# Experts' weights split into high and low parts in the experts' stage instead of beforehand, and position scatters in a chain

## The chip, the core and the metric
One Trainium2 chip, one of its cores. The metric is the device time of one execution in microseconds. Engines: PE (TensorE, matrix products), PEld (its weight loads), DVE (VectorE), ACT (ScalarE), POOL (GpSimd), SP (SyncE, which here issues nearly all DMAs).

## What is computed
Three layers in a row over 8 batches of 576 tokens, 4608 tokens of 512 numbers, all in 32-bit floating point.

```python
p_packed = sm_attn(p, k, v)                  # 32 packed queries per head attend to the keys
out = sm_attn(q, p_packed, p_packed)         # every token attends to the 32 packed rows
h = x @ w_in;  g = h * sigmoid(h);  x = g @ w_out          # 512 -> 2048 -> 512
e_idx = argmax(x @ w_gate)                                 # one of 8 experts for each token
gate = softmax(x @ w_gate)[e_idx] * sigmoid(x @ w_output_gate)[e_idx]
for e in range(8):                                         # 512 -> 1024 -> 512
    out[mask] = gate[mask] * (relu(x[mask] @ w1[e]) @ w2[e])
```

## The kernel before
**Products from two parts.** A matrix product in full precision is made of three products of rounded operands: a number is kept as a part rounded to the chip's type fp32r (hi) and the rest (lo), and lo x hi, hi x lo and hi x hi are summed in PSUM. Making the two parts of a tile takes two instructions: a copy on ACT that rounds (hi), and a subtraction on DVE (lo). This text calls the pair a rounding.

**Batches.** The first two layers run batch by batch (`batch`, L358). A batch has 16 steps, one for each 128 of the 2048 inner features. Step f issues in this order: the first product of step f (`mm1`, L690, into the PSUM buffer ps_h, of which there is one), the activation (`act`: tanh on ACT at L699, product g on DVE at L700, which frees ps_h), parts of other work by a schedule (`extra_steps`: attention of the next batch in pieces s1 to s9, the product m of the next weights with its m_lo at L672, and the routing of the batch before), the rounding of g (L705, L710, L717, L719), and the second product of step f-2 (`mm2`, L741). Every engine works through its own instructions in this order. In routing, `row_t` transposes the finished rows, `row_logits` and `row_logits2` make the experts' logits (the copy of lg at L290 reads ps_h), `finish` finds the best expert (mx, L764) and queues the gate's weights, and `place` works out each token's position among those of its expert and scatters token numbers there.

**Weights of the experts, beforehand.** From batch 1 to 6, `split_slot` (L505) is called in two of three steps: it takes a piece of w1 or w2 (128x1024, 512 KB) that SP has loaded, rounds it (ACT at L509, DVE at L510), and issues the load of another piece (`split_load`). `split_store` at the head of the next step writes both parts to the DRAM tensors ws1 and ws2. There are 64 pieces: 8 experts, two matrices, four pieces.

**Experts.** Tokens are handled in groups of 576 that have one expert; here there are 8 groups. Each group has 8 steps of 128 inner features, 64 steps in all, n = 0 to 63 (`groups`, L902). In step n the order is: up-projection of n+1 (`up`, L1011 on PE, relu at L1016 on ACT and its lo part at L1017 on DVE, again through one buffer ps_h), gap 2n+1, down-projection of n (`down`, L1033, L1036), gap 2n+2. A gap is a list of jobs put there by hand or by `plan`: transposes of the next group's rows (`trx`, L975 to L981), fetching the group after it (`fetch`: its expert's number, the token numbers from the DRAM table perm at L924 and L925, then five gathers of rows on POOL at L934), and loads of weights. `load_chunk` (L953) loads a quarter of an expert's weights, hi and lo of both matrices, 2 MB in two issues on SP (L959, L961), into a ring of five buffers; two belong to the pool qa, open since batch 7, three to the pool p2, which lies on memory of the batches and is opened as the experts begin. Chunks 0 and 1 are loaded in step 2 of batch 7 (`open_first`). The first group takes tokens of the first batches only, so its fetch begins in step 1 of batch 7.

**Position scatters.** `place` (L784) issues one indirect DMA on POOL for each 128 tokens (L809), 36 in all, four or five at a time. Before each one POOL clears a small tile (`spacer`), and `rows_apart` declares that they need not wait for each other. The loads at L924 and L925 read what they wrote. Four of the scatters are issued as the last batch ends and one in gap 3 of the experts.

Of the kernel before, what the change touches and what calls it, by code (L numbers as in the profile page):

```python
# [21 lines left out]
DM = 512  # L22
# [18 lines left out]
RING = 5  # L41
# [46 lines left out]
class Kernel:  # L88
    def __init__(self, tc, ins, out):
        self.tc, self.nc, self.i, self.out = tc, tc.nc, ins, out  # L90
        nc = tc.nc
        self.ws1 = nc.dram_tensor("ws1", (E8, 4, 2, 128, F2), F32, kind="Internal").ap()
        self.ws2 = nc.dram_tensor("ws2", (E8, 4, 2, 128, 2 * DM), F32, kind="Internal").ap()
        self.perm = nc.dram_tensor("perm", (PROWS, PW), I32, kind="Internal").ap()
        self.xr = nc.dram_tensor("xr", (NTOK + 1, XW), F32, kind="Internal").ap()
# [5 lines left out]
    def run(self):  # L101
# [19 lines left out]
        self.spacer = cp.tile([128, 1], I32, name="spacer")  # L121
# [16 lines left out]
        self.split_jobs = [(w, e, k) for e in range(E8) for w in (1, 2) for k in range(4)]  # L138
        self.split_n, self.split_raw, self.split_loaded, self.split_done = 0, [], [], []
        self.late, self.group = [], None  # L140
        self.ex, self.at, self.x, self.sc, self.hl, self.chunk = {}, {}, {}, {}, {}, {}
        self.xt, self.nload, self.banks = [None, None], 0, 2
# [6 lines left out]
        c_stg, self.stg = self.pool("spl", "right")  # L149
        for b in range(1, B - 1):  # L150
            self.batch(b)
        while self.split_jobs or self.split_loaded or self.split_done:
            self.split_store()
            self.split_slot()
        c_stg.close()
# [47 lines left out]
    def open_first(self, f):  # L203
        nc = self.nc
        if f == 1:
            self.ex[0] = nc.values_load(self.ptab[0:1, 0:1], engines=[ENG.SP], min_val=0, max_val=E8 - 1)
            xs = [self.p1.tile([128, 2, S], F32, tag=f"a2_0{i}", name="xs") for i in range(2)]
            self.fetch_ix(0, self.ptab[0:1, 1:2])
            og = xs[1][:, 1, :DM]
            nc.sync.dma_start(og, self.i["wog"][bass.ds(self.ex[0], 1), :].to_broadcast([128, DM]))  # L210
            mid = self.mid[:, 2 * DM:2 * DM + 2 * XW].rearrange("p (a b) -> p a b", a=2)
            self.x[0] = [*(x[:, :XW] for x in (xs[0][:, 0], xs[0][:, 1], xs[1][:, 0])), mid[:, 0], mid[:, 1]], og
        elif f == 2:
            self.load_chunk()
            self.load_chunk()
        elif f == 4:
            self.fetch_x(0)
        elif f == 13:
            t = self.pin.tile([128, 4 * FF], F32R, tag="w_in", name="xt0")
            self.xt[0] = t[:, :8 * GN].rearrange("p (h k t) -> p h k t", h=2, k=4)  # L220
            self.ring = t[:, 8 * GN:14 * GN].rearrange("p (i t) -> p i t", i=3)
# [136 lines left out]
    def batch(self, b, hook=None):  # L358
        sched = self.extra_steps(b)
        for f in range(NF):  # L360
            s = b * NF + f
            self.split_store()
# [13 lines left out]
            slot = 0 < b < B - 1 and (s - NF) % 3 < 2  # L376
            if slot and f != 1:
                self.split_slot()
# [3 lines left out]
            if slot and f == 1:  # L382
                self.split_slot()
# [18 lines left out]
            if b == 0 and f == 15:  # L402
                self.split_load()
                self.split_load()
# [92 lines left out]


    def split_store(self):
        for w, hi, dst in self.split_done:  # L500
            self.nc.sync.dma_start(dst[0], hi.bitcast(F32))
            self.nc.sync.dma_start(dst[1], w)
        self.split_done = []

    def split_slot(self):  # L505
        nc = self.nc
        for w, dst in self.split_loaded[:1]:
            hi = self.stg.tile([128, 1024], F32R, tag="shi", bufs=2, name="shi")
            nc.scalar.copy(out=hi, in_=w)  # L509
            nc.vector.tensor_tensor(out=w.bitcast(F32R), in0=w, in1=hi.bitcast(F32), op=ALU.subtract)  # L510
            self.split_done.append((w, hi, dst))
        self.split_loaded = self.split_loaded[1:]
        self.split_load()

    def split_load(self):
        nc = self.nc
        if not self.split_jobs:
            return
        which, e, k = self.split_jobs.pop(0)
        n = self.split_n  # L520
        self.split_n += 1
        if n < 3:
            self.split_raw.append(self.mid[:, (n + 1) * 1024:(n + 2) * 1024])
        elif n == 3:
            self.split_raw.append(self.stg.tile([128, 1024], F32, name="sw"))
        w = self.split_raw[n % 4]
        if which == 1:
            nc.sync.dma_start(w, self.i["w1"][e].rearrange("(k p) f -> p k f", p=128)[:, k, :])
            dst = self.ws1[e, k]
        else:  # L530
            nc.sync.dma_start(w.rearrange("p (k d) -> p k d", k=2),
                              self.i["w2"][e].rearrange("(k p) d -> p k d", p=128)[:, 2 * k:2 * k + 2, :])
            dst = self.ws2[e, k]
        self.split_loaded.append((w, dst))
# [249 lines left out]
    def place(self, g):  # L784
# [15 lines left out]
        def put():  # L800
# [6 lines left out]
            for r in range(n):  # L807
                nc.gpsimd.memset(self.spacer, 0)
                put = nc.gpsimd.indirect_dma_start(  # L809
                    out=self.perm, out_offset=bass.IndirectOffsetOnAxis(ap=di[:, r:r + 1], axis=0),  # L810
                    in_=self.tok[:, i0 + r:i0 + r + PW], in_offset=None)
                self.rows_apart("perm", put.ins)
# [57 lines left out]
    def more(self, lo, hi):  # L870
        self.nload = 4 * lo
        self.fetch(lo)
        for _ in range(4):
            self.load_chunk()
# [10 lines left out]
    def plan(self, lo, hi, first=5, every=2):  # L885
        for k in range(lo, hi - 1):
# [15 lines left out]
    def groups(self, lo, hi):  # L902
        self.gap(2 * FG * lo)
        for n in range(FG * lo, FG * hi):
# [10 lines left out]
            if n % 2 and n > 6 and self.nload < 4 * hi:  # L915
                self.load_chunk()
# [36 lines left out]
    def load_chunk(self):  # L953
        nc, n = self.nc, self.nload
        self.nload += 1
        slot, e, q = n % RING, self.expert(n // 4), n % 4
        t = (self.qa if slot < 2 else self.p2).tile([128, 4096], F32R, tag=f"w{slot}", name="w")
        f = t.bitcast(F32)
        nc.sync.dma_start(f[:, :2048].rearrange("p (a c) -> p a c", a=8),  # L959
                          self.ws1[bass.ds(e, 1), :, :, :, q * 256:q * 256 + 256].rearrange("e a b p c -> p (e a b) c"))  # L960
        nc.sync.dma_start(f[:, 2048:].rearrange("p (b c) -> p b c", b=2), self.ws2[bass.ds(e, 1), q].rearrange("e b p c -> p (e b) c"))  # L961
        self.chunk[n] = t
# [57 lines left out]
    def down(self, n, parts=None):  # L1020
# [3 lines left out]
        for n, j in parts:  # L1024
            g, ff = divmod(n, FG)
            w = self.chunk[n // 2][:, 2048:].rearrange("p (r k c) -> p r k c", r=2, k=2)[:, :, ff % 2, :]
# [65 lines left out]
```

## Time and profile before

| | us |
|---|---|
| median of 3 runs (lowest, highest) | 1271.96 (1271.86, 1272.64) |
| the profiled execution's own time | 1271.73 |
| its span, first to last instruction | 1269.6 |
| batches 1 to 6, about 140 to 736 us | 596 |
| batch 7 and the last rows, 736 to 834 us | 98 |
| experts, from 834 us | 425 to the last products, then 10 |

Mean granted clock of TensorE over the span: 0.984 of full speed. In the profile, L12 is line 12 of the kernel before; a name such as `acc<-wo,ghi` is the tile written and the tiles read. In a timeline a line is one instruction or several merged ones (x8): start in us from the span's first instruction, duration, engine, line, tiles, shape. What stands in brackets is the time that the engine had nothing to do before it and the instruction that ended that time; no bracket means no idle time. SPq lines are issues of DMAs. In the windows view a line is a stretch: its length, the busy us of PE, PEld, DVE, ACT and POOL with their numbers of instructions, the granted TensorE clock as a share of full speed, the mean busy share of the 16 DMA engines, and GB/s. A step number is f in `batch`; batches count from 0.

### The profile page before, as it was taken

What the parts mean: (1) busy time and instruction counts of PE and PEld (TensorE: products, weight loads), DVE (VectorE), ACT (ScalarE), POOL (GpSimd) and SP (SyncE); (2) the same over time, 40 slices, a digit from 0 to 9 for tenths busy, and PEclk for the clock granted to TensorE, in tenths of its full rate; (3) what the DMA queues carried; (4) which work ended last, traced back from release to release, by engine and by line L of the source; (5) the groups of instructions that cost most, each with busy time, mean ns of one, the idle gap of its engine ahead of it and who ended that gap; (6) DMA issues with size and microseconds to landing.
All of it is one profiled execution on the core that took longest, in us unless ns stands there. A gap on an engine that the chain in (4) does not pass through costs nothing. (4 is left out here: it accounts for less than half of the span.)

```text
span 1269.6 us, 22035 instructions
## 1 busy us (share of the span) xinstructions
PE 1204.2 (95%) x8760; PEld 998.4 (79%) x8760; DVE 656.2 (52%) x1495; ACT 472.9 (37%) x978; POOL 168.9 (13%) x211
## 2 busy tenths in 40 slices
PE   7697999999999999999999899999999999999996
PEld 3575887787777787787788778888999999999996
DVE  6889657456657556756645834433233232322311
ACT  3433554354554454464444433312221212212121
POOL 0234201000101000100000131013311303111011
PEclk9797999999999999999999999999999999999998
DMA  8555566565766656875845551069755656565411
GB/s 312 205 185 180 178 239 215 197 238 194 257 243 194 234 189 219 240 261 171 280 172 215 162 181 35 2 176 354 264 182 204 231 188 227 180 232 196 173 38 40
DMA packets 118725, 250.26 MB, mean 197 GB/s; under 512 B 13363, under 2 KB 64374, under 8 KB 118358
## 3 DMA queue, kind: packets, MB, share of 16 engines
q1 hardware_dynamic: 111318, 228.66, 53.1%
q0 software_dynamic: 7296, 20.11, 4.2%
q8 instruction: 71, 1.16, 0.4%
q14 instruction: 40, 0.33, 0.1%
HBM read 160.17 MB, written 88.70 MB: 196 GB/s over the span
## 5 line engine op out<-in xcount | busy, mean ns | idle before, releaser
L741 PE MATMUL acc<-wo,ghi 128*128 128x512 f32 x1024 | 320.7, 394 | 0.0
L741 PEld LDWEIGHTS acc<-wo,ghi 128*128 128x128 f32 x1024 | 194.4, 190 | 38.9
L1011 PE MATMUL pu<-xt,w 128*128 128x256 f32 (+1 forms) x1536 | 215.5, 296 | 0.0
L1011 PEld LDWEIGHTS pu<-xt,w 128*128 128x128 f32 x1536 | 209.6, 189 | 5.1
L741 PE MATMUL acc<-wo,glo 128*128 128x512 f32 x512 | 213.1, 416 | 0.0
L690 PE MATMUL ps_h<-a,m_hi 128*128 128x288 f32 x1024 | 212.1, 300 | 0.8 <-DVE a L656 0.8
L1017 DVE SCALAR_TENSOR_TENSOR xt<-pu,xt 128x512 fp32r<-128x512 f32 (+1 forms) x128 | 58.7, 458 | 294.9 <-ACT xt L1016 287.9
L1036 PE MATMUL py<-w,xt 128*128 128x512 f32 x768 | 187.7, 393 | 0.0
L690 PE MATMUL ps_h<-a,m_lo 128*128 128x288 f32 x512 | 161.8, 316 | 24.1 <-DVE g L700 17.2
L1016 ACT ACTIVATE xt<-pu 128x512 fp32r<-128x512 f32 (+1 forms) x128 | 52.7, 412 | 324.4 <-PE pu L1011 274.2
L1036 PEld LDWEIGHTS py<-w,xt 128*128 128x128 f32 x768 | 144.3, 188 | 33.0
L690 PEld LDWEIGHTS ps_h<-a,m_hi 128*128 128x128 f32 x1024 | 168.1, 193 | 2.5 <-DVE a L656 1.0
L700 DVE SCALAR_TENSOR_TENSOR g<-g,ps_h 128x576 f32<-128x576 f32 x128 | 96.1, 751 | 131.2 <-ACT g L699 130.8
L699 ACT ACTIVATE g<-ps_h 128x576 f32<-128x576 f32 x128 | 83.4, 652 | 171.8 <-PE ps_h L690 155.3
L690 PEld LDWEIGHTS ps_h<-a,m_lo 128*128 128x128 f32 x512 | 98.4, 192 | 50.4 <-DVE g L700 26.1
L741 PEld LDWEIGHTS acc<-wo,glo 128*128 128x128 f32 x512 | 97.3, 190 | 46.0 <-issue 27.0
L809 POOL DMA_INDIRECT perm<-tok,dsti x36 | 39.5, 1098 | 653.0 <-DVE dsti L805 516.7
L710 DVE TENSOR_TENSOR glo<-g,ghi 128x512 fp32r<-128x512 f32 x128 | 91.5, 715 | 38.2 <-ACT ghi L705 33.7
L705 ACT CAST ghi<-g 128x512 fp32r<-128x512 f32 x128 | 79.4, 620 | 74.1 <-DVE g L700 71.2
L510 DVE TENSOR_TENSOR mid<-mid,shi 128x1024 fp32r<-128x1024 f32 x48 | 58.8, 1226 | 43.3 <-ACT shi L509 43.3
L561 PE MATMUL ps_m<-w_in,ppt 64*32 64x256 f32 x1008 | 44.7, 399 | 9.2 <-ACT e L577 5.3
L509 ACT CAST shi<-mid 128x1024 fp32r<-128x1024 f32 x48 | 50.1, 1045 | 0.0
(188 smaller groups left out, 1155.8 us busy)
## 6 DMA issues: line engine op xcount, KB each, us to landing
w<-ws SPq DMA_DIRECT2D x64, 1024.0 KB
ws<-shi SPq DMA_DIRECT2D x64, 512.0 KB
mid<-in_w SPq DMA_DIRECT2D x48, 512.0 KB
ws<-mid SPq DMA_DIRECT2D x48, 512.0 KB
att_v<-in_v SPq DMA_DIRECT2D x15, 640.0 KB
att_k<-in_k SPq DMA_DIRECT2D x15, 576.0 KB
xr<-xr SPq DMA_DIRECT2D x32, 256.5 KB
stg<-in_w_in SPq DMA_DIRECT2D x16, 512.0 KB
```

The lines of the kernel that those rows point to most:

```text
L509: nc.scalar.copy(out=hi, in_=w)
L510: nc.vector.tensor_tensor(out=w.bitcast(F32R), in0=w, in1=hi.bitcast(F32), op=ALU.subtract)
L690: nc.tensor.matmul(ps[:, hf, :288], lw[:, qd, fs], rx[:, qd, ts], start=(i == 0), stop=(i == 5))
L699: nc.scalar.activation(out=g2, in_=ps[:, :, :288], func=AF.Tanh, scale=0.5)
L700: nc.vector.scalar_tensor_tensor(out=g2, in0=g2, scalar=1.0, in1=ps[:, :, :288], op0=ALU.add, op1=ALU.mult)
L705: self.nc.scalar.copy(out=hi, in_=self.graw[:, :512])
L710: self.nc.vector.tensor_tensor(out=lo, in0=self.graw[:, :512], in1=self.ghi.bitcast(F32), op=ALU.subtract)
L741: self.nc.tensor.matmul(acc, l, r, start=(first and i == 0), stop=(last and i == 2))
L1011: nc.tensor.matmul(ps[:, hf, :m], w[:, k, r, fs], xt[:, l, k, ts], start=(i == 0), stop=(i == 11))
L1016: nc.scalar.activation(out=hi, in_=src, func=AF.Relu)
L1017: nc.vector.scalar_tensor_tensor(out=lo, in0=src, scalar=0.0, in1=hi.bitcast(F32), op0=ALU.max, op1=ALU.subtract)
L1036: nc.tensor.matmul(self.acc[j], hl[:, l + j * 128:l + j * 128 + 128], w[:, r], start=(first and i == 0), stop=(last and i == 2))
```

## The change
The tensors ws1 and ws2, the roundings in batches 1 to 6 and their loads and stores go. The experts' stage loads quarters of w1 and w2 as they are given, 512 KB each, into two pairs of raw buffers (`load_raw`), and rounds them there (`split`) into a ring of three chunk buffers instead of five. Quarter q+2 is rounded in gaps 4q+2 (w1) and 4q+4 (w2), and quarter q+4 is loaded in gap 4q+4; quarter 0 is rounded in steps 7 and 9 of batch 7, quarter 1 in gaps 1 and 2. One chunk buffer now belongs to qa and two to p2. The layout of a chunk changes from part within matrix row to part first. The position scatters lose the spacer and the declaration, so each waits for the one before to have landed. The code for more than 8 groups (`more`) changes in the same way; it isn't reached here.

```diff
-RING = 5
+RING = 3
...
-        self.ws1 = nc.dram_tensor("ws1", (E8, 4, 2, 128, F2), F32, kind="Internal").ap()
-        self.ws2 = nc.dram_tensor("ws2", (E8, 4, 2, 128, 2 * DM), F32, kind="Internal").ap()
...
         elif f == 2:
-            self.load_chunk()
-            self.load_chunk()
+            self.load_raw(0)
+            self.load_raw(1)
         elif f == 4:
             self.fetch_x(0)
+        elif f == 7:
+            self.split(0, 1)
+        elif f == 9:
+            self.split(0, 2)
+            self.load_raw(2)
...
-            self.split_store()
             self.mm1(b, f)
...
-            slot = 0 < b < B - 1 and (s - NF) % 3 < 2
-            if slot and f != 1:
-                self.split_slot()
...
-            if slot and f == 1:
-                self.split_slot()
...
-                nc.gpsimd.memset(self.spacer, 0)
-                put = nc.gpsimd.indirect_dma_start(
+                nc.gpsimd.indirect_dma_start(
                     out=self.perm, out_offset=bass.IndirectOffsetOnAxis(ap=di[:, r:r + 1], axis=0),
                     in_=self.tok[:, i0 + r:i0 + r + PW], in_offset=None)
-                self.rows_apart("perm", put.ins)
...
-        self.gaps = {0: [lambda: self.row_t(g, 4), self.load_chunk], 1: [lambda: self.row_logits(g, 4)], 2: [lambda: self.place(g), self.load_chunk],
-                     3: [self.table], 5: [self.spread, lambda: self.fetch(1)], 11: [lambda: self.fetch(2)]}
-        for i in (8, 13, 14, 15):
-            self.gaps[i] = [self.load_chunk]
+        self.gaps = {0: [lambda: self.row_t(g, 4)], 1: [lambda: self.row_logits(g, 4), lambda: self.split(1, 1)],
+                     2: [lambda: self.place(g), lambda: self.split(1, 2), lambda: self.load_raw(3)], 3: [self.table],
+                     5: [self.spread, lambda: self.fetch(1)], 11: [lambda: self.fetch(2)]}
...
+        for q in range(4 * lo, 4 * hi - 2):
+            n = 4 * q + (4 if q == 0 else 2)
+            self.gaps.setdefault(n, []).append(lambda q=q: self.split(q + 2, 1))
+            self.gaps.setdefault(n + 2, []).append(lambda q=q: self.split(q + 2, 2))
+            if q + 4 < 4 * hi:
+                self.gaps[n + 2].append(lambda q=q: self.load_raw(q + 4))
...
-            if n % 2 and n > 6 and self.nload < 4 * hi:
-                self.load_chunk()
...
+    def load_raw(self, q):
+        nc, e, c = self.nc, self.expert(q // 4), q % 4
+        r1 = self.qa.tile([128, 4, 256], F32, tag="raw1", bufs=2, name="raw1")
+        r2 = self.qa.tile([128, 2, DM], F32, tag="raw2", bufs=2, name="raw2")
+        nc.sync.dma_start(r1, self.i["w1"][bass.ds(e, 1), :, c * 256:c * 256 + 256].rearrange("e (k p) f -> p (e k) f", p=128))
+        nc.sync.dma_start(r2, self.i["w2"][bass.ds(e, 1), c * 256:c * 256 + 256, :].rearrange("e (k p) d -> p (e k) d", p=128))
+        self.raw[q, 1], self.raw[q, 2] = r1, r2
+
+    def split(self, q, which):
+        nc, slot = self.nc, q % RING
+        if which == 1:
+            self.chunk[q] = (self.p2 if slot else self.qa).tile([128, 2, 2, 1024], F32R, tag=f"w{slot}", name="w")
+        hi, lo = [self.chunk[q][:, which - 1, r, :] for r in range(2)]
+        raw = self.raw.pop((q, which)).rearrange("p a b -> p (a b)")
+        nc.scalar.copy(out=hi, in_=raw)
+        nc.vector.tensor_tensor(out=lo, in0=raw, in1=hi.bitcast(F32), op=ALU.subtract)
...
-        w = self.chunk[n // 2][:, :2048].rearrange("p (k r c) -> p k r c", k=4, r=2)
+        w = self.chunk[n // 2][:, 0].rearrange("p r (k c) -> p k r c", k=4)
```

## Rows read from the trace of the kernel before

**Rows 1.** Windows view: busy time of each engine in two stretches.
```profile
140.00:736.00 596.00, 571.36 (x4658) 455.05 (x4657) 370.49 (x778) 290.87 (x559) 33.90 (x55) 1.00 0.64 216
834.00:1259.00 425.00, 425.00 (x2562) 385.68 (x2561) 126.75 (x387) 95.26 (x237) 74.04 (x86) 1.00 0.57 196
```

**Rows 2.** Waits of PE from 140 to 736 us: line, releaser, total us, times, longest.
```profile
PE ps_h L690 <- DVE g L700: 12.1, 15, 1.6
PE ps_s L561 <- DVE m_lo L672: 5.5, 5, 2.0
...
PE ps_h L690 <- DVE lg L290: 2.8, 6, 0.5
...
PE ps_h L690 <- DVE mx L764: 1.1, 2, 0.5
```

**Rows 3.** The roundings, groups of the page: busy us, mean ns (48 of 64 each).
```profile
L510 DVE TENSOR_TENSOR mid<-mid,shi 128x1024 fp32r<-128x1024 f32 x48 | 58.8, 1226 | 43.3 <-ACT shi L509 43.3
...
L509 ACT CAST shi<-mid 128x1024 fp32r<-128x1024 f32 x48 | 50.1, 1045 | 0.0
```

**Rows 4.** Timeline, step 12 of batch 4, then of batch 2: start, us, engine, line.
```profile
501.38 1.23 DVE L510 TENSOR_TENSOR sw<-sw,shi 128x1024 fp32r<-128x1024 f32 x1 [0.19 <-ACT shi L509]
...
505.29 0.40 PE L690 MATMUL ps_h<-a,m_lo 128*128 128x288 f32 x1 [0.61 <-DVE g L700]
...
307.72 0.29 PE L690 MATMUL ps_h<-a,m_lo 128*128 128x288 f32 x1
```

**Rows 5.** Timeline, PE at the change from batch 4 to 5.
```profile
539.72 0.40 PE L690 MATMUL ps_h<-a,m_lo 128*128 128x288 f32 x1 [1.46 <-DVE g L700]
```

**Rows 6.** Timeline, PE at step 13 of batch 1, then of batch 3.
```profile
213.06 0.72 PE L561 MATMUL ps_s<-att_q,ppt 64*32 64x288 f32 x16 [0.77 <-DVE m_lo L672]
...
408.19 0.72 PE L561 MATMUL ps_s<-att_q,ppt 64*32 64x288 f32 x16 [1.99 <-DVE m_lo L672]
```

**Rows 7.** Windows view, the stretch behind that wait; granted clock third from the end.
```profile
408.00:412.00 4.00, 3.81 (x29) 3.28 (x30) 2.57 (x6) 0.43 (x3) 1.67 (x4) 0.65 1.07 260
```

**Rows 8.** Timeline, DVE and PE at the second up-projection of the experts.
```profile
840.56 0.17 DVE L767 TENSOR_TENSOR oh<-cst,rt 128x8 bf16<-128x8 f32 x1
...
841.50 0.72 PE L1011 MATMUL pu<-xt,w 128*128 128x256 f32 x4
```

**Rows 9.** Timeline, a step of the experts: relu's last subtraction, next up-projection.
```profile
907.28 0.23 DVE L1017 SCALAR_TENSOR_TENSOR xt<-pu,xt 128x64 fp32r<-128x64 f32 x1 [0.29 <-ACT xt L1016]
...
909.07 1.12 PE L1011 MATMUL pu<-xt,w 128*128 128x256 f32 x8
```

**Rows 10.** Timeline of SP, and windows view, for one chunk's two loads.
```profile
929.82 0.37 SPq L959 DMA_DIRECT2D w<-ws  x1
...
938.00:938.50 0.50, 0.50 (x6) 0.50 (x5) 0.00 (x0) 0.00 (x0) 0.00 (x0) 1.00 0.02 8
```

**Rows 11.** Timeline of POOL, SP and PE: position scatters, index loads, gather, transposes.
```profile
731.18 0.96 POOL L809 DMA_INDIRECT perm<-tok,dsti  x1 [0.19 <-issue]
...
733.48 0.42 SPq L924 DMA_DIRECT2D xix<-perm  x1
...
832.31 0.96 POOL L809 DMA_INDIRECT perm<-tok,dsti  x1 [37.58 <-DVE dsti L805]
...
848.19 0.96 POOL L809 DMA_INDIRECT perm<-tok,dsti  x1 [11.01 <-DVE tb L825]
...
854.94 0.38 SPq L924 DMA_DIRECT2D xix<-perm  x1
...
857.78 0.98 POOL L934 DMA_INDIRECT xg<-xr,xix  x1 [8.49 <-issue]
...
867.59 0.60 PE L975 MATMUL px<-cst,xg 128*128 128x128 f32 x4
```

**Rows 12.** Timeline of POOL: a scatter beside a rounding's subtraction (batch 3).
```profile
403.80 1.72 POOL L809 DMA_INDIRECT perm<-tok,dsti  x1 [63.93 <-DVE dsti L805]
```

**Rows 13.** Timeline of PE: step 6 of batch 7.
```profile
756.26 0.37 PE L690 MATMUL ps_h<-a,m_lo 128*128 128x288 f32 x1 [0.42 <-DVE lg L290]
```

More of the change, by code (lines that the diff above doesn't have):

```diff
@@ L120, in run @@
         self.pick_i = cp.tile([128, 8], U32, name="pick_i")
-        self.spacer = cp.tile([128, 1], I32, name="spacer")
         self.ptab = cp.tile([1, 2], I32, name="ptab")
@@ L136, in run @@
         nc.gpsimd.memset(self.a1[0][64:128, 4, :], 0.0)
-        self.split_jobs = [(w, e, k) for e in range(E8) for w in (1, 2) for k in range(4)]
-        self.split_n, self.split_raw, self.split_loaded, self.split_done = 0, [], [], []
         self.late, self.group = [], None
-        self.ex, self.at, self.x, self.sc, self.hl, self.chunk = {}, {}, {}, {}, {}, {}
-        self.xt, self.nload, self.banks = [None, None], 0, 2
+        self.ex, self.at, self.x, self.sc, self.hl, self.chunk, self.raw = {}, {}, {}, {}, {}, {}, {}
+        self.xt, self.banks = [None, None], 2
         c_stg, self.stg = self.pool("stg", "right")
@@ L148, in run @@
         c_stg.close()
-        c_stg, self.stg = self.pool("spl", "right")
         for b in range(1, B - 1):
             self.batch(b)
-        while self.split_jobs or self.split_loaded or self.split_done:
-            self.split_store()
-            self.split_slot()
-        c_stg.close()
         c_att.close()
@@ L361, in batch @@
             s = b * NF + f
-            self.split_store()
             self.mm1(b, f)
@@ L381, in batch @@
                 self.mm2(*divmod(s - 2, NF))
-            if slot and f == 1:
-                self.split_slot()
             if wait and f == 1:
@@ L401, in batch @@
                 self.nc.sync.dma_start(self.wgt[:, :4 * E8].rearrange("p (k e) -> p k e", e=E8), self.i["wgt"])
-            if b == 0 and f == 15:
-                self.split_load()
-                self.split_load()
     def fill(self, b, conv, defer=False):
@@ L496, in split_out @@
         self.nc.gpsimd.tensor_tensor(out=self.wo[1][:, f, :], in0=w, in1=self.wo[0][:, f, :].bitcast(F32), op=ALU.subtract)
[L499 to L534, printed above, removed]
     def load_att(self, b, what, dst=None):
@@ L870, in more @@
     def more(self, lo, hi):
-        self.nload = 4 * lo
         self.fetch(lo)
-        for _ in range(4):
-            self.load_chunk()
+        for q in (4 * lo, 4 * lo + 1):
+            self.load_raw(q)
+            self.split(q, 1)
+            self.split(q, 2)
+        for q in (4 * lo + 2, 4 * lo + 3):
+            self.load_raw(q)
         for j in range(GB):
@@ L914, in groups @@
                 self.down(n)
-            if n % 2 and n > 6 and self.nload < 4 * hi:
-                self.load_chunk()
             self.gap(2 * n + 2)
@@ L951, in expert @@
         return self.ex[g]
[L953 to L962, printed above, removed]
+    def load_raw(self, q):
[13 more added lines that the diff above has]
+        nc.vector.tensor_tensor(out=lo, in0=raw, in1=hi.bitcast(F32), op=ALU.subtract)
     def trx(self, g, *js):
@@ L1025, in down @@
             g, ff = divmod(n, FG)
-            w = self.chunk[n // 2][:, 2048:].rearrange("p (r k c) -> p r k c", r=2, k=2)[:, :, ff % 2, :]
+            w = self.chunk[n // 2][:, 1].rearrange("p r (k c) -> p r k c", k=2)[:, :, ff % 2, :]
             hl = self.hl[n]
```

## The prediction

> **What bounds the kernel now.** I read the windows first: how much of each stage TensorE (PE) has nothing to do. In the six middle batches, 140 to 736 us, PE is busy 571.36 of 596.00 us, so 24.6 us are idle; in the experts' stage it is busy in all 425.00 us, while VectorE (DVE) and ScalarE (ACT) have 126.75 and 95.26 us of work there [rows 1]. So the batches can give back at most 24.6 us, and the experts can only lose. Second, the waits of PE in those batches: 12.1 us for the activation's product (g, L700), 5.5 us for m_lo, 3.9 us for lg and mx (2.8 and 1.1), nearly all the rest for x [rows 2]. All are DVE work. Third, the durations of what the change moves: the rounding of one 128x1024 piece is 1.045 us on ACT and 1.226 us on DVE [rows 3]. Fourth, the timeline around single waits, with and without a rounding ahead.
>
> **The roundings leave the batches.** 64 ACT casts, 64 DVE subtractions, 64 loads and 128 stores of 512 KB go from batches 1 to 6; on SP the attention loads are then no longer behind stores that wait for a rounding. The six batches are an experiment of their own: a rounding stands in two steps of three, so the same step has one in four batches and none in two.
> - Step 12 of batch 4: the subtraction starts at 501.38, the normalisation of q and the g product queue behind it on DVE, and PE waits 0.61 us before 505.29. The same step of batch 2 had no rounding, and there PE goes on at 307.72 without idle time [rows 4]. Steps 12 and 15 each have a wait in the four batches with a rounding and none in the two without; step 0 and step 3 show waits only behind one. Of the 15 g waits, three stand at a batch's change (at 342, 540 and 735 us, like the 1.46 us shown [rows 5]), where ACT waits for PE and no rounding is near: about 3 x 1.46 = 4.4 us stay. The gain is 12.1 - 4.4 = 7.7 us.
> - lg and mx, eight waits at steps 6 and 10 of 0.43 to 0.54 us: all have a rounding ahead of the copy, and the four such steps without one show no wait. Gain 3.9 us.
> - m_lo at step 13: 0.77 us without a rounding in an odd batch, 1.99 us with one [rows 6], no wait without one in an even batch. Keeping 0.77 us in each of three odd batches leaves 5.5 - 2.3 = 3.2 us of gain.
> - Behind the 1.99 us wait the granted clock is 0.65 of full speed for 4 us, part of them at 1.2 and the rest at 2.4 GHz [rows 7]; behind no other wait of these batches does it fall. 0.35 x 4 = 1.4 us come back.
>
> Together 7.7 + 3.9 + 3.2 + 1.4 = 16.2 us. The waits for x (about 3.1 us) I leave standing.
>
> **The roundings enter the last batch and the experts.** Chunk 0 is rounded at steps 7 and 9 of batch 7. Unseen there: between nothing and twice the 1.2 us by which a rounding lengthens a wait at most [rows 6]; batch 7 has less DVE work, so I take 0.5 us. Chunk 1 is rounded in gaps 1 and 2, since its buffer lies on memory freed just before. DVE is done with oh at 840.73, so the first subtraction ends at 840.73 + 1.23 = 841.96; the up-projection that reads it began at 841.50 [rows 8]. Cost 0.5 us, between nothing (cast and subtraction ahead of the oh chain) and 1.2 us. From chunk 2 on the cover is this: a step of the experts lasts 425/64 = 6.6 us, DVE has 2.0 us of work in it and ACT 1.5 us; 62 roundings in 64 steps make 3.2 and 2.5 us. They are issued in even gaps behind the relu and its subtraction, which end 1.56 us before the next up-projection needs their one PSUM buffer (907.51 against 909.07) [rows 9], and a rounding of 2.3 us issued then is over before the next relu is due. Cost nothing. If that cover went, each rounding could cost up to 2.3 - 1.56 = 0.7 us.
>
> **Loads.** The experts read 32 MB instead of 64, in 64 issues of 512 KB. The load of quarter q+4 waits on SP for the subtraction of q+2 (before, for the down-projection); its data are due three steps later, 3 x 6.6 - 2.3 = 17 us. Two issues of 1 MB each, begun at 929.82, had moved all by 938.50 [rows 10], 8.7 us for twice the bytes. Cost nothing. What queues behind the waiting SP are index and gate loads of a group two ahead.
>
> **The scatters wait for each other.** 36 memsets of 0.1 us go; each scatter now waits for the one before. One link, from start to landing, is at most 733.48 - 731.18 = 2.3 us where the load of the indices followed a last scatter, and at most 854.94 - 848.19 = 6.75 us at the experts' start, where that load also waited for the table [rows 11]. I take 2.3 us, as nothing else held that load. In the batches nobody is behind on POOL. The five scatters ahead of the first group's gathers delay these and the SP queue by some 5 us (28 at 6.75), against 50 us until their first use in steps 13 to 15 of batch 7. The four that begin at 832.31 end at 832.31 + 4 x 2.3 = 841.5, before the fifth is ready at 848.19; the gathers (857.78) and the transposes that use them (867.59) stay [rows 11]. Cost nothing. The Trainium skill, "DMA: Bandwidth & Descriptors", section "Anatomy of one DMA", gives about 2.0 us from issue to completion and says that a target in HBM can make it longer; by it a link would be about 3 us, the four would end at 844, and the sum would not change.
>
> **Sum.** -16.2 + 0.5 + 0.5 = -15.2 us. The profiled execution took 1271.73 us for a span of 1269.6; 1271.73 - 15.2 = 1256.5. It lies 0.23 us below the median of the three runs, which changes nothing here.
>
> **Rivals.**
> - *Only the g waits go.* The DVE chain moves up, but lg, m_lo and the clock stay as they are because other waits end at the same time: -7.7 + 1.0, **1265**. For it: 0.77 us stays without any rounding, and batch 7, which has none, waits 0.42 us at its steps 6 and 10 [rows 13]. Against: that batch lacks the attention work that stands between in the others, and their steps without a rounding show no wait.
> - *The second group's rows come late.* If a link is near 6.75 us the four scatters end at 859.3, the fifth starts 11.1 us later, and so do the gathers. They have 867.59 - 857.78 - 2.3 = 7.5 us to spare, so PE waits 3.6 us at the first transposes and 1.4 us go to the clock: **1261.5**. It decides from links of 5.9 us. On the same path a scatter that met the rounding's subtraction took 1.72 us instead of 0.96 [rows 12], and three roundings now lie beside the five gathers: up to 2.3 us more, within the 7.5. The Trainium skill, "SBUF — State Buffer", section "SBUF: two separate sides", says that GpSimd and a VectorE instruction with two SBUF inputs lock each other out of one port pair; the trace agrees.
> - *Nothing gained.* The roundings only mask waits that PE would meet one matmul later: **1271**. Against it again the steps without one.
> - *Slower: the raw quarters land late.* ACT works in order; a cast that waits for its data holds the relu queued behind it, that holds the down-projection, and PE stops. It decides where a load takes over 17 us from its issue. Each us beyond costs one us per quarter for 28 quarters; a load of 18 us gives 28.0 - 15.2 = 12.8 us more than now, **1285**. For it: the ring shrinks from five to three, and w1 arrives in runs of 1 KB. Against it: 8.7 us for twice the bytes.
>
> **How the numbers follow.** Forecast 1256.5 with chance 0.58; only g 0.13; late second group 0.09; nothing gained 0.09; slower 0.11. Two versions within 0.2%, 2.5 us, can hardly be told apart. Faster is 0.58 + 0.13 + 0.09 = 0.80, same 0.09, slower 0.11. Low end: the waits for x and the three of 0.77 us go too, 1256.5 - 3.1 - 2.3 = 1251. The high end, 1267, takes in the first two rivals and the upper bounds of the two unseen costs (1.9 and 0.7 us more). What lies outside is the last two rivals, 0.20.
>
> **What would show it.** Right: PE idle in the six batches near 10 us; g waits only at the three batch changes; no clock dip near 408; the experts at 100% but for half a us at the second up-projection; the scatters some 2.3 us apart. Wrong: PE waits behind relu or its subtraction in each expert step, casts on ACT that wait for DMA, or a wait at the first transposes after 867 us (shifted).

## The result, and the profile after

The changed kernel takes 1242.34 us (median of 4 runs, 1242.06 to 1242.94), the kernel before 1271.91 us beside it (4 runs, 1271.15 to 1272.64): 29.6 us less, ratio 0.9768, 95% interval 0.9751 to 0.9785. The forecast was 1256.5 us, 1251 to 1267: the right direction, half the size, outside the range.

The windows view of the changed kernel, with the same two stages as [rows 1] (us, then busy us of PE, PEld, DVE, ACT and POOL; at the end granted clock, DMA share, GB/s):

```profile
140.00:706.00 566.00, 564.15 (x4657) 454.49 (x4656) 297.02 (x715) 232.00 (x495) 24.97 (x25) 1.00 0.19 51
804.00:1229.00 425.00, 424.96 (x2560) 384.74 (x2561) 199.58 (x449) 153.05 (x298) 84.37 (x82) 1.00 0.39 120
```

The experts' stage takes the same 425 us and PE is still busy all of it, with 73 us more on DVE than before (199.58 against 126.75) and 58 more on ACT. All the gain lies in the six batches, which take 566 us in place of 596: PE idles 1.85 us there where it idled 24.64. Of the waits shown in [rows 2] none is left; all that the view of waits names is half of the waits for x:

```profile
PE ps_m L509 <- DVE x L577: 1.6, 3, 0.5
```

The groups of the page for the two halves of a rounding (busy us, mean ns, idle time before):

```profile
L920 DVE TENSOR_TENSOR w<-raw,w 128x1024 fp32r<-128x1024 f32 x64 | 78.2, 1223 | 27.5 <-ACT w L919 25.8
L919 ACT CAST w<-raw 128x1024 fp32r<-128x1024 f32 x64 | 67.3, 1053 | 0.0
```

A rounding's two halves take what [rows 3] showed. The up-projection of step 12 of batch 4 waits for the product g of step 11. It now starts on DVE 0.84 us behind the end of its tanh, and PE goes on without a wait; in the kernel before DVE reached g only 2.25 us behind the tanh, and PE waited [rows 4]. DVE before, DVE after, then PE after:

```profile
504.49 0.75 DVE L700 SCALAR_TENSOR_TENSOR g<-g,ps_h 128x576 f32<-128x576 f32 x1
```

```profile
487.57 0.75 DVE L648 SCALAR_TENSOR_TENSOR g<-g,ps_h 128x576 f32<-128x576 f32 x1
```

```profile
489.01 0.29 PE L638 MATMUL ps_h<-a,m_lo 128*128 128x288 f32 x1
```

At the change from batch 4 to 5 the wait of 1.46 us [rows 5], which the forecast left standing, is gone too:

```profile
520.51 0.29 PE L638 MATMUL ps_h<-a,m_lo 128*128 128x288 f32 x1
```

**Where the 29.6 us came from.** I followed the end of each step's up-projection in both profiles. The lead of the changed kernel, the time by which it is ahead, is -0.3 us at the start of batch 1, 29.6 at step 15 of batch 7, and from 29.3 to 29.6 through the experts. By the kind of wait that stood there before:

```
kind (waits)                    forecast   measured   of it idle time in the rows
g, steps 12, 15, 0, 3 (12)         7.7       11.2         7.8
g, three batch changes (3)         0          5.2         4.4
lg and mx, steps 6 and 10 (8)      3.9        4.2         3.9
m_lo, step 13 (5), with clock      4.6        7.0         5.5
x                                  0          1.9         1.5
batch 7, second up-projection     -1.0        0           -
```

These make 29.5 of the 29.6 us. Two things show. Of three kinds of waits that the forecast kept or kept in part, two are gone and half of the third (x), and a wait for g was worth more than its idle time. The second is read from one step: the wait at step 12 of batch 4 has 0.61 us of idle time [rows 4]. The tanh of steps 11 and 13 on ACT, before and then after:

```profile
501.59 0.65 ACT L699 ACTIVATE g<-ps_h 128x576 f32<-128x576 f32 x1 [0.24 <-PE ps_h L690]
...
513.22 0.65 ACT L699 ACTIVATE g<-ps_h 128x576 f32<-128x576 f32 x1 [1.87 <-PE ps_h L690]
```

```profile
486.08 0.65 ACT L647 ACTIVATE g<-ps_h 128x576 f32<-128x576 f32 x1 [1.20 <-PE ps_h L638]
...
496.81 0.65 ACT L647 ACTIVATE g<-ps_h 128x576 f32<-128x576 f32 x1 [3.33 <-PE ps_h L638]
```

Across that wait the lead grows from 501.59 - 486.08 = 15.51 to 513.22 - 496.81 = 16.41 us, so 0.90 us for 0.61 idle. All fifteen waits for g give 0.27 to 0.31 us beyond their idle time. They stand where PE's stream of matmuls had run empty; the view counts from the modelled end of the last matmul, and the stream has to fill again: the first matmul of that up-projection takes 0.40 us [rows 4], in the changed kernel 0.29. The eight waits for lg and mx give only 0.03 to 0.04 us more. In front of them the stream is broken in the changed kernel too, as at step 10 of batch 4, where the same matmul takes 0.40 us with no wait ahead of it:

```profile
478.97 0.40 PE L638 MATMUL ps_h<-a,m_lo 128*128 128x288 f32 x1
```

The Trainium skill, "TensorE: Matmul & The Clock Gate", section "Single matmul latency", gives for a single bf16 matmul a fixed part of some 0.17 us at the upper clock. These fp32 matmuls lose 0.28 us at a wait for g, so they agree in kind only.

### The profile page after: what moved, and what is told of

Same layout as the page of the kernel before. It is cut to its first block, busy times and chain, and to the rows that moved or that the text cites. A ratio compares the mean times of both kernels' runs of the same rounds, so it can differ in the third digit from the quotient of the medians.

```text
span 1240.7 us, 21632 instructions
## 1 busy us (share of the span) xinstructions
PE 1198.9 (97%) x8758; PEld 999.6 (81%) x8760; DVE 657.4 (53%) x1495; ACT 474.1 (38%) x978; POOL 171.1 (14%) x175
## 4 chain that ended last, share of the span: by engine, by line
PE 77%; DVE 10%; issue 8%; ACT 2%; DMA 1%; POOL 1%; SPq 0%; POOLq 0%; DVEq 0%; ACTq 0%
PE acc L689 26%; PE ps_h L638 14%; PE pu L969 13%; PE py L994 10%; PE accL L689 3%; PE ps_m L509 2%; PE py L991 2%; PE ps_rt L249 1%; PE px L933 1%; PE ps_s L509 1%; DVE glo L658 1%; DVE wf L467 1%; DVE wf L470 1%; DMA spare<-in_q 1%; POOL out L1011 1%
## 5 line engine op out<-in xcount | busy, mean ns | idle before, releaser
L756 POOL DMA_INDIRECT perm<-tok,dsti x36 | 36.1, 1002 | 630.9 <-DVE dsti L753 450.1
L920 DVE TENSOR_TENSOR w<-raw,w 128x1024 fp32r<-128x1024 f32 x64 | 78.2, 1223 | 27.5 <-ACT w L919 25.8
L919 ACT CAST w<-raw 128x1024 fp32r<-128x1024 f32 x64 | 67.3, 1053 | 0.0
```

What stands on the lines that cost most here:

```text
L919: nc.scalar.copy(out=hi, in_=raw)
L920: nc.vector.tensor_tensor(out=lo, in0=raw, in1=hi.bitcast(F32), op=ALU.subtract)
```

## The experiments

The time of the kernel before differs by chip: 1271.9 us in the first comparison, 1271.6 and 1271.5 on two chips of the experiments (kind one), 1266.8, 1266.1 and 1267.2 on three others (kind two). Each of these chips was met on one occasion, so chip and occasion can't be told apart. Each run is held against the kernels on its own kind of chip.

### What the roundings cost in the batches

**a_round**: the changed kernel with the work of the 64 roundings put back, on data that lie in SBUF.

```diff
+            if slot and f != 1:
+                self.split_slot()
...
+        hi = self.stg.tile([128, 1024], F32R, tag="shi", bufs=2, name="shi")
+        nc.scalar.copy(out=hi, in_=w)
+        nc.vector.tensor_tensor(out=w.bitcast(F32R), in0=w, in1=hi.bitcast(F32), op=ALU.subtract)
```

> The changed kernel with 64 casts and 64 subtractions of 128x1024 put back at the old places in batches 1 to 6, on pieces that lie in SBUF and are thrown away: no loads, no stores, scatters that wait for each other. If the time that the roundings take on DVE and ACT is the cause of all waits but the three at batch changes: 1242.3 + 24.5 = 1266.8, with the waits of the kernel before at steps 6, 10 and 12 to 15. If part of those waits needs the loads and stores (a rounding that waits for its data, a store that holds the attention loads): less than 1266, and the missing steps show which.

1267.0 us (kind two), ratio 1.0006 to the kernel before (0.9997 to 1.0015). Its waits of PE in the batches, without a byte loaded or stored for it:

```profile
PE ps_h L657 <- DVE g L667: 8.1, 11, 1.3
PE ps_s L528 <- DVE m_lo L639: 5.6, 5, 2.0
PE ps_h L657 <- DVE lg L287: 2.8, 6, 0.5
PE ps_m L528 <- DVE x L596: 2.0, 3, 0.7
PE ps_rl L268 <- DVE x L596: 1.1, 2, 0.7
PE ps_h L657 <- DVE mx L731: 1.1, 2, 0.5
```

These are [rows 2] over again, but for the three waits at batch changes; step by step the profile agrees with that of the kernel before on this kind of chip (before_again, below) to 0.12 us, apart from steps 13 to 15 of batch 3, where up to 0.7 us more is lost. The engine work alone makes the 24 us.

**b_traffic**: the kernel before without the roundings, each piece stored twice as it came; 64 loads and 128 stores stay.

```diff
-            nc.scalar.copy(out=hi, in_=w)
-            nc.vector.tensor_tensor(out=w.bitcast(F32R), in0=w, in1=hi.bitcast(F32), op=ALU.subtract)
-            self.split_done.append((w, hi, dst))
+            self.split_done.append((w, w, dst))
```

> The kernel before without the 64 casts and 64 subtractions in the batches; the 64 loads and 128 stores stay, each piece stored twice as it came (the kernel leaves out the splitting into two parts, so its products lack the second part). Scatters in a burst as before. If the roundings' time on DVE and ACT is the cause of all waits but the three at batch changes, and the burst the cause of these three: 1271.9 - 24.7 = 1247.2, PE waits only there. If the roundings cause those three as well: 1242. If the loads and stores slow the attention loads, the matmuls or the vector work themselves: 1255 to 1272, with waits that stay at steps 12 to 15.

1241.61 us (kind two). The windows view from 140 to 707 us:

```profile
140.00:707.00 567.00, 565.17 (x4676) 455.37 (x4671) 297.08 (x715) 233.36 (x498) 31.45 (x55) 1.00 0.68 227
```

PE idles 1.8 us beside 227 GB/s. The traffic costs nothing. **b_traffic_serial**, the same with scatters that wait for each other (the place function of the changed kernel):

> As the run with loads and stores but no roundings, and with scatters that wait for each other. If loads and stores cost nothing by themselves, and burst and roundings are all: 1242.3, the time of the changed kernel, with PE idle under 3 us from 140 us to the end of batch 6. If the traffic costs something by itself, that is what stands above 1242.3. If the three waits at the batch changes come from the traffic alone and not from the burst: 1247.5, the same as with the burst.

1243.75 us: its profile loses 1.4 us on that of b_traffic, all at the transposes of the second group of rows; the section on the scatters comes back to that.

**a_cast** and **a_sub**: a_round without the subtraction, and without the cast (its first cast alone stays).

```diff
-        nc.vector.tensor_tensor(out=w.bitcast(F32R), in0=w, in1=hi.bitcast(F32), op=ALU.subtract)
```

> The changed kernel with only the 64 casts of 128x1024 put back on ACT. DVE theory: nearly nothing comes back, 1242 to 1245. ACT theory: over half of 24.5, above 1254. If the two add up over the chain from ACT to DVE, the two runs share the 24.5 us.

a_cast takes 1243.35 us, and loses nothing in the batches (0.7 of the 0.9 us by which its profile lies above that of after_again stands ahead of batch 1): ACT has 58 us more to do than in the changed kernel on the other kind of chip, PE is busy to 0.01 us the same. First a_cast, then the changed kernel (**after_again**, below), 140 to 707 us:

```profile
140.00:707.00 567.00, 565.18 (x4663) 455.52 (x4662) 297.16 (x715) 290.79 (x559) 24.70 (x26) 1.00 0.20 53
```

```profile
140.00:707.00 567.00, 565.19 (x4665) 455.60 (x4664) 296.86 (x716) 232.70 (x496) 24.94 (x26) 1.00 0.19 51
```

> The changed kernel with only the 64 subtractions of 128x1024 put back on DVE at the old places of batches 1 to 6 (thrown away), no casts on ACT. If DVE's queue alone makes the waits, as I read the rows of the kernel before (PE waits for g, lg, mx and m_lo, all written by DVE): nearly all of the 24.5 us come back, 1264 to 1267, with waits at steps 6, 10 and 12 to 15. If the cast ahead of each subtraction is what delays (ACT holds tanh and the cast of g): under half, below 1254.

1258.83 us, some 16.5 us over the changed kernel: below what I expected, above the rival. Its two largest waits of PE in the batches:

```profile
PE ps_s L530 <- DVE m_lo L641: 5.2, 5, 2.0
PE ps_h L659 <- DVE g L669: 3.4, 7, 0.9
```

m_lo waits as in a_round, g far less (8.1 us there). Subtractions alone cost 16.5 us, casts alone nothing, both together 24: some 8 us come only from the pair. In a_round DVE stands still until the cast ahead of its subtraction is done, with the next work of the chain queued behind; in a_sub this wait is 0.3 us in all. That the 8 us are this standing is read from the waits and was not tried by itself. DVE in a_round:

```profile
DVE mid L502 <- ACT shi L501: 50.4, 58, 12.6
```

**a_round_mid**: a_round with 48 roundings at steps 1 to 5 and 7 to 9.

```diff
+            slot = 0 < b < B - 1 and f in (1, 2, 3, 4, 5, 7, 8, 9)
```

> The changed kernel with 48 roundings (cast and subtraction of 128x1024, thrown away) put back in batches 1 to 6, all at steps 1 to 5 and 7 to 9, eight in each batch; the run with 64 had them at two steps of three. There the roundings at these steps left the lead of the kernel without them unchanged, and all of the 24 us was lost at steps 6, 10 to 15 and 0. If it is the place that decides (the chain of DVE at steps 10 to 15 has no room, the others have): 1242.3 to 1243.5. If it is the amount of DVE and ACT work: three quarters of 24.5, 1260.

1249.67 us: neither. The waits name the difference:

```profile
PE ps_h L657 <- DVE lg L287: 4.2, 9, 0.5
...
PE ps_h L657 <- DVE mx L731: 1.6, 3, 0.5
```

Of 6.6 us in its profile 6.2 are lost at steps 6 and 10, 0.46 to 0.58 us in each of the twelve. A rounding at step 5 or 9 delays lg or mx in the next step, for which PE's up-projection waits. At the other six steps 36 roundings cost at most the 0.4 us that is left. The place decides, and a rounding reaches one step further than it stands.

### The scatters and the batch changes

At the change from batch 4 to 5 PE waits for g because its tanh on ACT starts late, 1.7 us after ACT was free. Five scatters in a burst, 1.27 us apart, lie in the same microseconds of the kernel before; the last:

```profile
535.97 0.96 POOL L809 DMA_INDIRECT perm<-tok,dsti  x1 [0.19 <-issue]
```

**b_serial**: the kernel before with the scatter part of the change alone. **a_burst**: the changed kernel with the old scatters. (The spacer's memsets go and come with the burst in all these runs and were not tried by themselves.)

```diff
-                nc.gpsimd.memset(self.spacer, 0)
-                put = nc.gpsimd.indirect_dma_start(
+                nc.gpsimd.indirect_dma_start(
...
-                self.rows_apart("perm", put.ins)
```

> The kernel before with one part of the change alone: the position scatters wait for each other (no spacer, no promise that rows are apart); roundings, loads and stores stay in the batches. Theory A (the burst of five scatters holds back the signals of PE to ACT, and that is the wait of 1.46 us at three batch changes): the tanh of step 1 in batches 3, 5 and 7 follows its matmuls within 0.2 us, the three waits of PE at 342, 540 and 735 us go, and with 0.28 us of refilling behind each the time falls by 3 x (1.46 + 0.28) = 5.2 us, to about 1266.7. Theory B (those waits come from the roundings or from the loads and stores): the three waits stay and the time is 1271.9. Theory C, my blind forecast for this part (scatters cost and give nothing): 1271.9 too, or up to 2 us slower where the longer chain holds the index loads.

> The changed kernel with the old scatters put back (spacer of 0.1 us between them, no waiting for each other); no roundings, loads or stores in the batches. Theory A in its simple form (the burst alone holds the signals): 1242.3 + 5.2 = 1247.5, with tanh late by 1.7 to 2.8 us at step 1 of batches 3, 5 and 7. Theory A with a condition (the burst does it only beside the loads and stores of 512 KB): 1242.3, no late tanh. Theory B: 1242.3.

On chips of kind two: 1268.39 us against 1266.82, ratio 1.0013 (1.0004 to 1.0022), and 1242.62. Neither has a late tanh, and by these two no theory of the batch changes could be told from another. The rise of b_serial is the rival that I had priced, the second group's rows. Its scatters at the experts' start on POOL, the wait at the first transposes on PE, and the windows behind it:

```profile
827.41 0.96 POOL L807 DMA_INDIRECT perm<-tok,dsti  x1 [32.32 <-DVE dsti L804]
837.09 0.96 POOL L807 DMA_INDIRECT perm<-tok,dsti  x1 [8.72 <-DMA perm<-tok,dsti]
842.56 0.96 POOL L807 DMA_INDIRECT perm<-tok,dsti  x1 [4.51 <-DMA perm<-tok,dsti]
849.84 0.96 POOL L807 DMA_INDIRECT perm<-tok,dsti  x1 [6.32 <-DMA perm<-tok,dsti]
852.70 0.96 POOL L807 DMA_INDIRECT perm<-tok,dsti  x1 [1.90 <-DMA perm<-tok,dsti]
```

```profile
864.92 0.66 PE L972 MATMUL px<-cst,xg 128*128 128x128 f32 x4 [2.04 <-DMA xg<-xr,xix]
```

```profile
864.00:868.00 4.00, 3.08 (x18) 3.08 (x19) 0.69 (x1) 0.58 (x1) 0.00 (x0) 0.72 1.02 391
868.00:872.00 4.00, 4.00 (x23) 3.73 (x23) 0.69 (x1) 0.85 (x3) 1.77 (x2) 0.86 1.08 332
```

The links are 9.7, 5.5, 7.3 and 2.9 us long, the last scatter starts 9.0 us later than in before_again (843.66), PE waits 2.04 us and the clock stands at 0.72 and 0.86 for 4 us each: 0.28 x 4 + 0.14 x 4 = 1.7 us more. In the changed kernel the first three links are 6.2, 2.4 and 4.5 us; the last scatter then waits for DVE's tb, and so stands where it would stand without them:

```profile
802.69 0.96 POOL L756 DMA_INDIRECT perm<-tok,dsti  x1 [31.55 <-DVE dsti L753]
808.85 0.96 POOL L756 DMA_INDIRECT perm<-tok,dsti  x1 [5.20 <-DMA perm<-tok,dsti]
811.22 1.45 POOL L756 DMA_INDIRECT perm<-tok,dsti  x1 [1.40 <-DMA perm<-tok,dsti]
815.71 0.96 POOL L756 DMA_INDIRECT perm<-tok,dsti  x1 [3.05 <-DMA perm<-tok,dsti]
818.67 0.96 POOL L756 DMA_INDIRECT perm<-tok,dsti  x1 [2.00 <-DVE tb L771]
```

**before_again** and **after_again**: both kernels unchanged, on a chip of kind two.

> The kernel before, unchanged, for a second profile. On the chip of the experiments its median was 1266.8 us, 5.1 us less than the 1271.9 us of the first comparison. Theory A2 (the three late tanh at the batch changes, with the burst of scatters beside the roundings, happen on one chip or in one alignment and not in the other): here the tanh of step 1 in batches 3, 5 and 7 follows its matmuls within 0.2 us, and everything else stands as in the first profile: 1271.9 - 5.2 = 1266.7. Rival (the whole chip is a little faster): late tanh as before, and the 5 us spread over all stages.

> The changed kernel, unchanged, on the chip of the experiments. Under theory A2 the changed kernel has no late tanh to lose, so it takes 1242.3 here as in the first comparison, and the gain on this chip is 1266.8 - 1242.3 = 24.5 us instead of 29.6. Rival (a faster chip): 1242.3 - 5 = 1237.3.

1267.39 us (one run) and 1242.10 us. Step by step the second profile of the kernel before differs from the first at one kind of place: 5.3 us at step 2 of batches 3, 5 and 7, 0.5 us in the step behind. ACT at the change to batch 5 in the first profile and in the second:

```profile
535.89 0.64 ACT L577 COPY e<-ps_s 128x576 f32<-128x576 f32 x1 [2.44 <-DVE sm L576]
538.22 0.65 ACT L699 ACTIVATE g<-ps_h 128x576 f32<-128x576 f32 x1 [1.70 <-PE acc L741]
```

```profile
534.65 0.64 ACT L577 COPY e<-ps_s 128x576 f32<-128x576 f32 x1 [2.02 <-DVE sm L576]
535.19 0.66 ACT L699 ACTIVATE g<-ps_h 128x576 f32<-128x576 f32 x1
```

In the first the matmuls of that step end at 535.5 and ACT is free at 536.5, but tanh starts at 538.22. The trace has no completion signal of PE between 535.02 and 538.14 us, and then five within 0.21 us, one for the up-projection and four for down-projection blocks whose matmuls end 0.7 us apart. In the second profile they come 0.7 us apart. At all three batch changes of the first profile the held signals come 2.0 to 2.2 us after the start of the burst's fifth scatter (here 538.14 - 535.97 = 2.17 us). The bursts of four scatters in the same profile hold none.

**a_round_burst**: a_round and a_burst in one.

> As the run with the roundings put back, and with the scatters in a burst. If burst and roundings together make the late tanh at step 1 of batches 3, 5 and 7: 1266.8 + 5.2 = 1272. If loads and stores are needed for it, or if it belongs to the other chip: 1266.8.

1267.75 us, no late tanh, but again on kind two. Then four of them met a chip of kind one (kernel before there 1271.54 us):

> The scatter part of the change alone, once more. It decides where the kernel before takes 1271 to 1273 us (the chip shows the late tanh at three batch changes); where it takes 1266 this repeats what is known. On a chip of the first kind, burst theory: the three late tanh go (5.2 us) and the second group's rows come late as in the first run of this kernel (3.5 us): about 1270.2, no tanh of step 1 more than 0.2 us behind its matmuls. Rival (the burst has no part in it): late tanh stay and the second group's rows come late: 1275.

> Loads, stores and burst without roundings, once more, for the same question. On a chip of the first kind: if burst and the loads and stores make the late tanh without any rounding, 1241.6 + 5.2 = 1246.8; if a rounding is needed, 1241.6.

> Roundings and burst without loads and stores, once more, for the same question. On a chip of the first kind: if burst and roundings make the late tanh without the loads and stores, 1267 + 5.2 = 1272; if the loads and stores are needed, 1267.

> The burst alone, once more, for the same question. On a chip of the first kind: 1242.3 + 5.2 = 1247.5 if the burst alone makes the late tanh there, else 1242.3.

```
                                             kind two    kind one
burst  before (roundings, traffic)            1266.1      1271.5
burst  a_round_burst (roundings)              1267.8      1273.0
burst  b_traffic (traffic)                    1241.6      1248.4
burst  a_burst (neither)                      1242.6      1248.7
waits  b_serial (roundings, traffic)          1268.4      1268.8
waits  changed kernel (neither)               1242.1      1242.3
```

The four with a burst take 5.2 to 6.8 us more on kind one, the two without stay within 0.4 us. On that kind the burst alone does it: a_burst_2 has neither roundings nor traffic, and loses 4.8 us at the three batch changes in its profile. At the change to batch 5 its DVE, then its PE:

```profile
522.15 0.76 DVE L525 TENSOR_REDUCE sm<-ps_s 128x2 f32<-128x576 f32 x1 [3.87 <-PE acc L690]
```

```profile
518.32 0.72 PE L510 MATMUL ps_s<-att_k,att_p 64*32 64x288 f32 x16
...
525.03 0.40 PE L639 MATMUL ps_h<-a,m_lo 128*128 128x288 f32 x1 [1.47 <-DVE g L649]
```

The matmuls that sm reads end at 519.04, DVE starts 3.1 us later, and PE then waits 1.47 us for g, as in [rows 5]. The two that were to tell the burst from everything else, b_serial_2 and a_burst_2, give 2.8 us off (ratio to the kernel before 0.9978, 0.9968 to 0.9987) and 6.4 us on (against the changed kernel of the first comparison; it was not run on that chip). In b_serial_2 the profile shows the 5.2 us of the batch changes gained and 1.8 us given back at the second group's rows. Why one chip holds the signals back and another does not stays open.

### The cover in the experts

**a_split2** and **a_split4**: each rounding of chunks 2 to 31 done twice and four times.

```diff
+        for _ in range(2 if q > 1 else 1):
             nc.scalar.copy(out=hi, in_=raw)
             nc.vector.tensor_tensor(out=lo, in0=raw, in1=hi.bitcast(F32), op=ALU.subtract)
```

> The changed kernel with each rounding of chunks 2 to 31 in the experts' stage done twice (same result). Each step then has 2.0 + 2 x 1.22 = 4.4 us of DVE work and 1.5 + 2 x 1.05 = 3.6 us of ACT work against 6.6 us of PE work, and the pair issued behind the relu's subtraction is over 1.05 + 2 x 1.22 = 3.5 us later, before the next relu is due some 5.5 us after it. Cover theory: 1242.3, PE busy all through. If the second half of the step has less room than I read (an up-projection held 0.7 us in each step): 1242.3 + 60 x 0.7 = 1284.

> The same with each rounding done four times: 2.0 + 4 x 1.22 = 6.9 us of DVE work in a step of 6.6 us. Cover theory: the cover is used up, DVE becomes the bound, at least 60 x 0.3 = 18 us slower, 1260 or more. If it stays at 1242, a rounding in the experts costs DVE less than its duration says.

1257.99 us and 1506.29 us. My 3.5 us for the pair was wrong: the second cast writes what the first subtraction reads, so it waits for it, and ACT can do nothing else meanwhile. ACT in a_split2, then PE in a_split2 and in a_split4 (experts' stage):

```profile
ACT w L920 <- DVE w L921: 74.7, 52, 1.6
```

```profile
PE pu L970 <- DVE xt L976: 9.3, 8, 2.2
```

```profile
PE pu L970 <- DVE sc L952: 54.0, 20, 4.0
PE pu L970 <- DVE xt L976: 48.5, 14, 9.8
```

So the pair is a chain of 2 x (1.05 + 1.22) = 4.5 us, and an ordinary step covers it. The 15.7 us of a_split2 are not spread over the 60 roundings. In its profile 7.4 us are lost in steps 4 to 8, as the experts begin, and 1.0 to 2.2 us at one step of each later group; the other 48 steps from step 9 on lose at most 0.05 us each. At the step shown here, step 18, ACT first writes out the results of the group before, which it does once a group, and the casts queue behind that. The windows view from step 11 on, then ACT and PE at such a step:

```profile
880.00:1230.00 350.00, 344.73 (x2068) 310.72 (x2066) 222.44 (x397) 176.72 (x295) 66.51 (x59) 1.00 0.37 115
```

```profile
921.70 2.42 ACT L1004 ACTIVATE y<-py,sc 128x512 f32<-128x512 f32 x4
```

```profile
929.92 3.43 PE L970 MATMUL pu<-xt,w 128*128 128x256 f32 x24 [0.86 <-DVE xt L976]
```

Four roundings are a chain of 9.1 us in a step of 6.6, and cost 264 us, 4.4 each, with a granted clock of 0.86 over the stage. One rounding, 2.3 us, is covered in an ordinary step with at least 2.2 us to spare, and in every step of the changed kernel; the cover that the forecast named is there.

## Why the prediction was wrong

- **"The roundings leave the batches", the mechanism: right.** DVE's queue makes the waits (a_sub 16.5 us, a_cast 0, a_round all 24; the 8 us between need the cast that a subtraction waits for), and loads and stores cost nothing (b_traffic). The experts, batch 7's roundings and the second up-projection cost nothing as well; the two charges of 0.5 us did not come, and batch 7 keeps its own waits ([rows 13]: 0.42 us, still there).
- **The gain of the g waits, 7.7 us: mis-sized.** The idle time was read rightly (7.8 of it went), but each wait was worth 0.28 us more for the refilling, a term that the forecast did not have: 3.4 us in all.
- **"The three waits at a batch's change stay": this step failed.** They went, for 5.2 us. "Where ACT waits for PE and no rounding is near" was a right reading of the row, and a reason to look for what held PE's signal. I took a wait that I could not explain for one that the change would not touch. The scatters stood in the same microseconds on POOL, and I costed them at nothing because nobody was queued behind them there; their burst held back PE's signal (a_burst_2, b_serial_2).
- **"Cost nothing" for the scatters: wrong in sign on chips of kind one, right for the changed kernel on kind two.** The link was put at 2.3 us, with 6.75 as its upper end. At the experts' start the links of the changed kernel lie between 2.4 and 6.2 us and those of b_serial reach 9.7; in the batches they reach 8.1 and 9.3 us: beside traffic the upper end was too low. The Trainium skill, "DMA: Bandwidth & Descriptors", section "Anatomy of one DMA", gives a fixed cost of about 2.0 us. The estimate of about 3 us a link that the forecast made from it comes near only in quiet stretches (2.4 us). The rival of the late second group was a true mechanism (b_serial, 3.5 us in its profile); the changed kernel, which loads half as much in that stage, escapes it. That the loads are the reason was not tried by itself.
- **"Keeping 0.77 us in each of three odd batches": failed.** The 0.77 us was read at step 13 of batch 1, where no rounding stands in step 11. But one stands in step 10, and a_round brings this wait back. Its subtraction pushes back the whole chain of DVE ahead of m_lo: the product g of step 12 starts at 211.65 us and in the changed kernel at 209.65, 2.0 us earlier, where PE's lead is 1.2. My comparison of steps with and without a rounding took the step as the unit, and a rounding reaches further, as a_round_mid shows at steps 6 and 10. The same goes for the x waits that I left standing, of which half went. DVE before (twice), then after, in batch 1:

```profile
202.94 1.23 DVE L510 TENSOR_TENSOR sw<-sw,shi 128x1024 fp32r<-128x1024 f32 x1 [0.31 <-ACT shi L509]
...
211.65 0.75 DVE L700 SCALAR_TENSOR_TENSOR g<-g,ps_h 128x576 f32<-128x576 f32 x1
```

```profile
209.65 0.75 DVE L648 SCALAR_TENSOR_TENSOR g<-g,ps_h 128x576 f32<-128x576 f32 x1
```

- **The clock: right in size.** 1.4 us were forecast; over steps 13 and 14 of batch 3, behind the wait at 408 us, the lead grew by 3.4 us for 1.99 us of idle time, so by 1.4 us more.

Without the three batch changes the gain is 24.0 us (1266.13 to 1242.10 on kind two), still over the forecast of 15.2 us and over the 20.7 us of its low end: the refilling and the other waits left standing are enough to miss.

## What to carry to other kernels

Before a wait is left standing, find out what holds its releaser; "no part of the change is near" is to be checked on every engine and queue in those microseconds, POOL's scatters too. Price a wait of TensorE at its idle time plus, where it breaks a dense stream of matmuls, the refilling; a lead taken step by step against an undisturbed step shows which (0.28 us at the waits for g, 0.04 at those for lg). And ask of a piece of side work on an in-order engine at which step it stands and which it reaches: 36 roundings at quiet steps cost at most 0.4 us here, 64 spread evenly 24 us.

## What the runs showed of the hardware

- Five indirect scatters issued 1.27 us apart held back completion signals of PE by up to 2.6 us, until 2.0 to 2.2 us after the fifth had started, on two of the chips whose profile was read, and not on others; the matmuls went on meanwhile. In no profile with scatters that wait for each other did it happen.
- A scatter took 2.4 us from its start to the start of the next where little else moved (3 to 10 GB/s), up to 9.7 us beside the loads at the experts' start (b_serial), and up to 11.2 us beside the loads and stores of the batches (b_serial_2).
- A wait for g cost PE about 0.28 us beyond the idle time in its row, a wait for lg or mx 0.04 us.
- Casting twice into one tile made ACT wait 74.7 us, 52 times, for the subtraction that still read it (a_split2).
